# Attention's transfers pinned to program order and placed earlier, its memory branch a step later, token tiles in two stages

## The chip, the core and the metric

One core of a Trainium2 chip runs one program. The metric is device time in microseconds (us) of one execution, from launch to the end; lower is better. TensorE (PE) does matmuls, VectorE (DVE), ScalarE (ACT) and GpSimd (POOL) do the elementwise work, and SyncE (SP) issues almost every DMA transfer. Each engine works through its own queue in order.

## The reference, cut to what matters

```
q, k, v: [4, 8, 576, 64];  M_prev: [4, 8, 64, 64];  z_prev: [4, 8, 64]
scores = q k^T / 8, causal;  a = softmax(scores);  local = a v
phi(x) = where(x > 0, x, exp(x) - 1) + 1
mem_out = (phi(q) M_prev) / (phi(q) . z_prev + 1e-6)
x = g * mem_out + (1 - g) * local        # g = sigmoid(beta), per head
x = reshape(x) to [2304, 512]
x = relu(x w_in)^2 w_out                 # 512 -> 2048 -> 512
out = mixture of 8 experts over x        # each token to one expert, capacity 288
```

w_in and w_out arrive as 64-bit floats and are turned into 32-bit ones on the chip.

## The kernel before

Attention works on pairs of heads: 4 batches of 4 pairs, numbered n = 0 to 15. `step(n)`, for n = -2 to 16, has ten places u = 0 to 9 and carries several pairs at once: `trans` transposes the probabilities of pair n (at each u), `score` makes those of pair n + 1 (at u = 1, 3, 5, 7, 8), `prep_q` and `prep_k` split q and k of pair n + 2 into a high and a low part (u = 4 and 8), `prep_v` does so for v of pair n (u = 2), `prep_m` transposes phi(q) of pair n (u = 1 and 3), and `read` makes the attention output (the pair's first columns at u = 4 and 8, the rest at u = 0 and 1 of the next step, after which it is stored to `x_d` in DRAM). `PLAN` lists these places. `phi(n)` is the memory branch: two ACT instructions write `e`, one DVE instruction `qp`, POOL multiplies by `zb` (z_prev on all partitions), DVE reduces that to `nr`, POOL scales `qp`. The tiles `e`, `qp`, `zb`, k and v have one buffer each, q has two.

Between these pieces `fill` puts matmuls of the first pass over the feed-forward layer (`Ffn.first`), from step 4 on: `FILLS` and `BEFORE` say how many at each place, 60 in a whole step. That pass goes by 8 tiles of 288 tokens. `tokens(i)` loads tile i from `x_d` in four chunks of 128 features (`xf`, two buffers), POOL adds the two halves of each, ACT and DVE split it into `xs` (one buffer), and `xs` is stored to `xs_d` for the later passes. Then 72 matmuls make the hidden layer of 6 chunks (`hidden`), and 72 more the output in 4 pieces d (`output`), each of which ACT copies to `yo` (two buffers) and SP stores to `yp_d`. Tile i can begin when its batch has been stored (`ended` sets `have`): tiles 0 and 1 from step 4 on, 2 and 3 from step 8, 4 and 5 from step 12, 6 and 7 at the end. `CONVERT` puts two conversions of a weight chunk (`fetch`, then `narrow` and `split`) into each of steps 0 to 5.

PE follows the program's order. The order on the other engines, and on SP's queue, is set by a scheduler that walks the program with a model of the times and issues what is ready, earlier traced work first. `keep_in_program_order` ties one instruction behind the one traced before it on its engine. Before the change it is used for the weight fetches of the first pass and for the first ACT instruction of their conversion, and for nothing else: all other transfers go where the scheduler puts them. So `phi(n + 2)`, traced at u = 1 of step n, cannot write `qp` before `prep_m` of pair n + 1 has been through PE, a step later.

Of the kernel before, what the change touches and what calls it, by code (L numbers as in the profile page):

```python
# [7 lines left out]
F32 = mybir.dt.float32  # L8
# [20 lines left out]

def narrow(nc, f, tmp, raw):  # L30
# [5 lines left out]
    a = nc.scalar.activation(tmp.bitcast(F32), high.bitcast(F32), AF.Copy, scale=2.0 ** -112)  # L36
# [3 lines left out]
    return a  # L40
# [9 lines left out]
def attention(tc, ident, q, k, v, M_prev, z_prev, beta, x_d, fill, ended):  # L50
# [5 lines left out]
    with ExitStack() as ctx:  # L56
# [13 lines left out]
        def load(n, names="qkv"):  # L70
            b, hp = divmod(n, HP)
            for nm, src in (("q", q), ("k", k), ("v", v)):
# [4 lines left out]
                for j in range(2):  # L77
                    nc.sync.dma_start(dst[:, 0:4, j, :],
                                      src[b, 2 * hp + j, 0:512, :].rearrange("(t p) d -> p t d", p=128))
                for to, r in ends:  # L80
                    nc.sync.dma_start(to[r:r + 64, 4], src[b, 2 * hp:2 * hp + 2, 512:576, :].rearrange("h p d -> p h d"))
# [3 lines left out]
        nc.sync.dma_start(g, beta[None, :].to_broadcast([128, H]))  # L85
# [26 lines left out]
        MB, zb = {}, {}  # L112

        def load_norm(b):
            zb[b] = one.tile([128, DM], F32, name="zb")
            nc.sync.dma_start(zb[b], z_prev[b].rearrange("h d -> (h d)")[None, :].to_broadcast([128, DM]))

        def load_memory(n):
            b, hp = divmod(n, HP)
            raw = two.tile([128, 2, 64], F32, name="mraw")  # L120
            for j in range(2):
                nc.sync.dma_start(raw[64 * j:64 * j + 64], M_prev[b, 2 * hp:2 * hp + 2].rearrange("h d e -> d h e"))
            m = MB[n] = two.tile([128, 2, 128], F32R, name="mb")
            split(nc, m[:, :, 0:64], m[:, :, 64:128], raw)
# [41 lines left out]
        def phi(n):  # L166
            b, hp = divmod(n, HP)
            if hp == 0:
                load_norm(b)
# [8 lines left out]
                                    zb[b][:, None, 128 * hp:128 * hp + 128].to_broadcast([128, 5, 128]), op=OP.mult)  # L178
# [119 lines left out]
        def read(n, c, j):  # L298
# [18 lines left out]
            if c == 1 and j == 1:  # L317
                xo = XO.pop(n)
                for s in range(2):
                    nc.sync.dma_start(x_d[s, 128 * hp:128 * hp + 128, b * S:b * S + S].rearrange("(j d) t -> d j t", j=2),  # L320
                                      xo[64 * s:64 * s + 64])

        def step(n):
# [3 lines left out]
            for u in range(10):  # L327
                if has[1]:
                    trans(n, u)
# [4 lines left out]
                for what in PLAN[u]:  # L334
# [960 lines left out]
```

## Time and profile before

| | us |
|---|---|
| median of 3 runs | 1049.72 (1047.99 to 1050.88) |
| profiled execution, its own time | 1049.03 |
| span from first to last instruction in it | 1047.3 |
| attention's steps alone, until the first pass's matmuls join | about 0 to 120 |
| attention's steps with the first pass beside them | about 120 to 369 |
| rest of the first pass | about 369 to 424 |
| later passes, then the mixture of experts | 424 to the end |

The span is what the views below divide. What is outside it (1.7 us) is launch and end.

### The profile page before, as it was taken

The page shows a single profiled execution, that of the slowest core. Times are in us where ns is not written, and L with a number is a line of the kernel's source. Part 1 is how long each engine was busy: PE and PEld are TensorE (multiplying, and loading weights), DVE is VectorE, ACT ScalarE, POOL GpSimd, SP SyncE. Part 2 cuts the span into 40 slices and gives each one's busy share as a digit, 9 for nine tenths or more (in the row PEclk, how much of TensorE's full clock was granted, in tenths as well). Part 3 has the DMA queues.
Part 4 walks back from the last instruction along what each step waited for, and adds up shares of the span by engine and source line. Part 5 has one row for each costly group of instructions (what it writes and reads, how often), then busy time and mean ns, then how long its engine had stood idle before and what let it go on. Part 6 is the DMA issues. An engine that isn't in the chain of part 4 may idle for free.

```text
span 1047.3 us, 19732 instructions
## 1 busy us (share of the span) xinstructions
PE 959.4 (92%) x7017; PEld 879.1 (84%) x7017; DVE 655.2 (63%) x1925; ACT 552.6 (53%) x1370; POOL 540.3 (52%) x535
## 2 busy tenths in 40 slices
PE   5777879999999988999999999999598999999996
PEld 3666668988889987999999999877498888989996
DVE  6889888888888737256427943335775567674110
ACT  6778878888888735444322343431252453344531
POOL 4666776766666525344312121211394865687841
PEclk9778889999999999999999999999698999999999
DMA  6345736374526277769583332101542444437400
GB/s 154 106 123 142 192 89 179 75 196 100 172 67 175 56 233 227 220 223 315 185 293 122 117 125 83 68 12 41 193 162 79 152 184 151 156 130 258 147 28 27
DMA packets 150724, 150.75 MB, mean 144 GB/s; under 512 B 71641, under 2 KB 122841, under 8 KB 150497
## 3 DMA queue, kind: packets, MB, share of 16 engines
q1 hardware_dynamic: 147552, 140.05, 43.6%
q0 software_dynamic: 3072, 9.44, 2.9%
q8 instruction: 55, 0.90, 0.4%
q14 instruction: 45, 0.36, 0.1%
HBM read 111.69 MB, written 37.77 MB: 143 GB/s over the span
## 4 chain that ended last, share of the span: by engine, by line
PE 61%; DVE 12%; issue 7%; DMA 6%; ACT 6%; POOL 5%; SPq 1%; POOLq 0%; DVEq 0%; ACTq 0%
PE ph L1066 12%; PE ph L45 6%; PE ph L46 6%; PE ph L47 6%; PE py L45 4%; PE py L46 4%; PE py L47 4%; PE ps L312 3%; POOL wsp L1050 3%; PE ps L217 3%; PE ps L271 2%; PE rs L843 2%; DMA raw<-in_moe_w_out_dram 1%; DMA raw<-in_moe_w_in_dram 1%; ACT P L240 1%
## 5 line engine op out<-in xcount | busy, mean ns | idle before, releaser
L489 POOL TENSOR_TENSOR gf<-r 128x384 f32<-128x384 f32 (+1 forms) x108 | 87.4, 810 | 206.9 <-ACT r L487 198.1
L1050 POOL TENSOR_TENSOR wsp<-wraw,wsp 128x1024 fp32r<-128x1024 f32 x64 | 150.9, 2393 | 42.8 <-ACT wsp L1048 31.6
L26 DVE TENSOR_TENSOR gs<-gf,gs 128x384 fp32r<-128x384 f32 (+1 forms) x108 | 65.6, 607 | 91.4 <-ACT gs L25 90.9
L1066 PE MATMUL ph<-xs,wsp 128*128 128x288 f32 x768 | 120.0, 306 | 0.0
L1066 PE MATMUL ph<-hs,wsp 128*128 128x288 f32 x768 | 117.5, 307 | 0.0
L246 POOL TENSOR_SCALAR P<-P,R,og 128x128 f32<-128x128 f32 (+2 forms) x144 | 99.5, 707 | 24.6 <-DVE R L244 17.7
L1066 PEld LDWEIGHTS ph<-xs,wsp 128*128 128x128 f32 x768 | 106.6, 192 | 3.6 <-issue 2.8
L1066 PEld LDWEIGHTS ph<-hs,wsp 128*128 128x128 f32 x768 | 107.2, 194 | 0.9 <-DVE hs L1090 0.4
L1048 ACT ACTIVATE wsp<-wraw 128x1024 fp32r<-128x1024 f32 x64 | 64.0, 1051 | 48.6 <-DMA wraw<-in_moe_w_dram 29.1
L487 ACT ACTIVATE r<-ph 128x384 f32<-128x384 f32 (+1 forms) x108 | 48.6, 450 | 77.6 <-PE ph L47 76.5
L240 ACT ACTIVATE P<-P,R 128x128 f32<-128x128 f32 (+2 forms) x144 | 83.4, 580 | 8.4 <-DVE R L228 6.9
L25 ACT ACTIVATE gs<-gf 128x384 fp32r<-128x384 f32 (+1 forms) x108 | 52.5, 486 | 58.0 <-POOL gf L489 49.6
L45 PE MATMUL ph<-xt,win 128*128 128x384 f32 x240 | 81.3, 339 | 0.0
L46 PE MATMUL ph<-xt,win 128*128 128x384 f32 x240 | 80.8, 337 | 0.0
L47 PE MATMUL ph<-xt,win 128*128 128x384 f32 x240 | 80.7, 336 | 0.0
L45 PE MATMUL ph<-xs,win 128*128 128x288 f32 x192 | 64.3, 335 | 10.6 <-ACT r L487 7.6
L271 PE MATMUL ps<-ident,P 128*128 128x128 f32 x320 | 62.3, 302 | 8.6 <-DVE R L228 3.3
L46 PE MATMUL py<-gs,wout 128*128 128x384 f32 x192 | 64.7, 338 | 0.3 <-DVE gs L26 0.3
L47 PE MATMUL py<-gs,wout 128*128 128x384 f32 x192 | 63.9, 336 | 0.0
L26 DVE TENSOR_TENSOR ptb<-ps,ptb 128x384 fp32r<-128x384 f32 (+3 forms) x128 | 59.1, 464 | 7.4 <-ACT ptb L25 5.8
L45 PE MATMUL py<-gs,wout 128*128 128x384 f32 x192 | 63.4, 338 | 0.0
L228 DVE CUSTOM_DVE_ANT_0 P<-ps,maskw 128x128 f32<-128x128 f32 (+3 forms) x128 | 58.5, 483 | 6.2 <-PE ps L217 3.2
(259 smaller groups left out, 2596.4 us busy)
## 6 DMA issues: line engine op xcount, KB each, us to landing
wraw<-in_moe_w_dram SPq DMA_DIRECT2D x32, 1024.0 KB, 5.5
xt<-xs_d SPq DMA_DIRECT2D x12, 1536.0 KB, 7.2
x_d<-xo SPq DMA_DIRECT2D x32, 288.0 KB, 3.8
xf<-x_d SPq DMA_DIRECT2D x32, 288.0 KB, 3.8
xs_d<-xs SPq DMA_DIRECT2D x8, 1152.0 KB, 6.6
raw<-in_moe_w_in_dram SPq DMA_DIRECT2D x16, 512.0 KB, 5.4
raw<-in_moe_w_out_dram SPq DMA_DIRECT2D x16, 512.0 KB, 5.5
yp<-yo SPq DMA_DIRECT2D x32, 144.0 KB, 3.9
```

Of the source, the lines that this page charges most:

```text
L26: (eng or nc.vector).tensor_tensor(lo, src, hi.bitcast(F32), op=OP.subtract)
L45: nc.tensor.matmul(out, lhi, rhi, start=start, stop=False)
L46: nc.tensor.matmul(out, lhi, rlo, start=False, stop=False)
L47: nc.tensor.matmul(out, llo, rhi, start=False, stop=stop)
L228: nc.vector.tensor_tensor_reduce(out=pw, in0=ps[:, 0:W[u]], in1=maskw[:, 512 - 128 * t:640], op0=OP.add, op1=OP.min, scale=-0.125, scalar= ...
L240: nc.scalar.activation(pw, pw, AF.Exp, bias=R[:, 0, u:u + 1], scale=-1.0, accum_out=R[:, 1, u:u + 1])
L246: nc.gpsimd.tensor_scalar(PP[n][w], PP[n][w], R[:, 2, w:w + 1], og9[:, hp, w:w + 1], op0=OP.mult, op1=OP.mult)
L271: nc.tensor.transpose(tr[:, 128 * i:128 * i + 128], P[:, 128 * i:128 * i + 128], ident)
L489: nc.gpsimd.tensor_tensor(gf, r, r, op=OP.mult)
L1048: nc.scalar.activation(w[:, 0, hs], raw[:, hs], AF.Copy)
L1050: eng.tensor_tensor(w[:, 1, hs], raw[:, hs], w[:, 0, hs].bitcast(F32), op=OP.subtract)
L1066: nc.tensor.matmul(out, l[a], r[b], start=i + p == 0, stop=i == n - 1 and p == 2)
```

## The change

1. **Transfers pinned.** A helper `transfer` issues a DMA and ties it behind the SP instruction traced before it. It is used for the loads of q, k, v, beta, z_prev and M_prev, the store to `x_d`, and, as long as attention runs, for the loads of `xf` and the stores of `xs_d` and `yp_d`.
2. **Places.** The loads stood after the step; now q of pair n + 3 stands at u = 5, k at u = 6, v of pair n + 1 at u = 7, M_prev and z_prev of pair n + 1 at u = 0. The load of M_prev is apart from its split (`prep_memory`, u = 4).
3. **Memory branch.** `phi(n + 1)` stands at u = 4 where `phi(n + 2)` stood at u = 1.
4. **z_prev by pairs.** A tile of 128 columns per pair (16 loads) in place of one of 512 per batch (4 loads).
5. **Token tiles in two stages.** Stage 0 loads and adds chunks 0 and 1; stage 1 splits them, then loads, adds and splits chunks 2 and 3. For the next tile stage 0 stands after the fourth hidden chunk and stage 1 at the start of the output; where the batch is not stored by then, they stand at output pieces 2 and 3. Tile 0 does one, 4 calls of waiting, the other, 4 more. Before, the whole stood at output piece 2, tile 0's at the start with 8 calls of waiting. The store to `xs_d` moves behind the second hidden chunk.
6. **Conversions.** The first ACT instruction is no longer tied, it writes a buffer of its own (`rc`) instead of `r`, which the hidden layer uses too, and the first fetch stands in step -1.

```diff
+def transfer(tc, out, src, pinned=True):
+    a = tc.nc.sync.dma_start(out, src)
+    if pinned:
+        tc.keep_in_program_order(a)
...
-        MB, zb = {}, {}
-
-        def load_norm(b):
-            zb[b] = one.tile([128, DM], F32, name="zb")
-            nc.sync.dma_start(zb[b], z_prev[b].rearrange("h d -> (h d)")[None, :].to_broadcast([128, DM]))
+        MB, MR, zb = {}, {}, {}
+
+        def load_norm(n):
+            b, hp = divmod(n, HP)
+            zb[n] = one.tile([128, 128], F32, name="zb")
+            transfer(tc, zb[n], z_prev[b, 2 * hp:2 * hp + 2].rearrange("h d -> (h d)")[None, :].to_broadcast([128, 128]))
         def load_memory(n):
             b, hp = divmod(n, HP)
-            raw = two.tile([128, 2, 64], F32, name="mraw")
+            raw = MR[n] = two.tile([128, 2, 64], F32, name="mraw")
             for j in range(2):
-                nc.sync.dma_start(raw[64 * j:64 * j + 64], M_prev[b, 2 * hp:2 * hp + 2].rearrange("h d e -> d h e"))
+                transfer(tc, raw[64 * j:64 * j + 64], M_prev[b, 2 * hp:2 * hp + 2].rearrange("h d e -> d h e"))
+
+        def prep_memory(n):
             m = MB[n] = two.tile([128, 2, 128], F32R, name="mb")
-            split(nc, m[:, :, 0:64], m[:, :, 64:128], raw)
+            split(nc, m[:, :, 0:64], m[:, :, 64:128], MR.pop(n))
...
@@ step(n)
+                if u == 0 and has[2]:
+                    load_memory(n + 1)
+                if u == 0 and has[2]:
+                    load_norm(n + 1)
+                if u == 5 and n + 3 < np_:
+                    load(n + 3, "q")
+                if u == 6 and n + 3 < np_:
+                    load(n + 3, "k")
+                if u == 7 and has[2]:
+                    load(n + 1, "v")
...
-                    if what == "p" and has[3]:
-                        phi(n + 2)
+                    if what == "p" and has[2]:
+                        phi(n + 1)
                     if what == "q" and has[2]:
-                        load_memory(n + 1)
+                        prep_memory(n + 1)
...
-            if n + 3 < np_:
-                load(n + 3, "qk")
-            if 0 <= n + 1 < np_:
-                load(n + 1, "v")
...
-CONVERT = {0: (10, 0), 1: (10, 0), 2: (10, 0), 3: (10, 0), 4: (10, 0), 5: (4, 10)}
+CONVERT = {-1: (10,), 0: (10, 0), 1: (10, 0), 2: (10, 0), 3: (10, 0), 4: (10, 0), 5: (4, 10)}
-PLAN = (("b0",), ("b1", "m0", "p"), ("v",), ("m1",), ("q", "k0", "a0"), (), (), (), ("k1", "a1"), ())
+PLAN = (("b0",), ("b1", "m0"), ("v",), ("m1",), ("p", "q", "k0", "a0"), (), (), (), ("k1", "a1"), ())
...
@@ weights(...)
-        t_ = (psum or self.two).tile([128, DM], I32, name="pr" if psum and psum is self.p2x else "r")
+        if first:
+            t_ = self.start.tile([128, DM], I32, name="rc")
+        else:
+            t_ = (psum or self.two).tile([128, DM], I32, name="pr" if psum and psum is self.p2x else "r")
...
@@ tokens(i)
-        xs = self.start.tile([128, 2, KD, TB], F32R, name="xs")
-        for kk in range(KD):
-            xf = self.start.tile([128, 2, TB], F32, name=f"xf{kk % 2}")
-            nc.sync.dma_start(xf, self.x_d[:, 128 * kk:128 * kk + 128, TB * i:TB * i + TB].rearrange("s p t -> p s t"))
-            nc.gpsimd.tensor_tensor(xf[:, 0], xf[:, 0], xf[:, 1], op=OP.add)
-            split(nc, xs[:, 0, kk], xs[:, 1, kk], xf[:, 0])
-        nc.sync.dma_start(self.xs_d[:, :, :, TB * i:TB * i + TB], xs.bitcast(F32))
-        return xs
+        def load(ks):
+            for kk in ks:
+                xf[kk] = self.start.tile([128, 2, TB], F32, name=f"xf{kk % 2}")
+                transfer(self.tc, xf[kk], self.x_d[:, 128 * kk:128 * kk + 128, TB * i:TB * i + TB].rearrange("s p t -> p s t"),
+                         self.yout is None)
+                nc.gpsimd.tensor_tensor(xf[kk][:, 0], xf[kk][:, 0], xf[kk][:, 1], op=OP.add)
+        def parts(ks):
+            for kk in ks:
+                split(nc, xs[:, 0, kk], xs[:, 1, kk], xf[kk][:, 0])
+        xf = {}
+        load((0, 1))
+        yield
+        xs = self.xs[i] = self.start.tile([128, 2, KD, TB], F32R, name="xs")
+        parts((0, 1))
+        load((2, 3))
+        parts((2, 3))
+        yield
@@ first(gpool)
-        nc, xs, cs = self.nc, {}, PASSES[0]
+        nc, cs, at, way = self.nc, PASSES[0], [0] * (NB_T + 1), {}
+        def ahead(i, stage):
+            if i < NB_T and self.have > i and at[i] == stage:
+                way.setdefault(i, self.tokens(i))
+                next(way[i])
+                at[i] += 1
         for i in range(NB_T):
             while self.have <= i:
                 yield 0
-            if i not in xs:
-                xs[i] = self.tokens(i)
-                for _ in range(LAG):
+            while at[i] < 2:
+                ahead(i, at[i])
+                for _ in range(LAG // 2):
                     yield 0
-            G = {}
+            xs, G = self.xs[i], {}
             for c in cs:
-                G[c] = yield from self.hidden(xs[i], c, gpool)
+                G[c] = yield from self.hidden(xs, c, gpool)
+                if c == cs[1]:
+                    transfer(self.tc, self.xs_d[:, :, :, TB * i:TB * i + TB], xs.bitcast(F32), self.yout is None)
+                if c == cs[3]:
+                    ahead(i + 1, 0)
             for ds in ((0, 1), (2,), (3,)):
-                if ds[0] and i + 1 < NB_T and i + 1 not in xs and self.have > i + 1:
-                    xs[i + 1] = self.tokens(i + 1)
+                ahead(i + 1, 0 if ds[0] == 2 and not at[i + 1] else 1)
...
@@ apart(...)
-        raws = []
+        raws = [f.fetch(c, part, pool, f"raw{n}") for n, (part, c) in enumerate(todo[:1])]
+        yield
```

## Rows read from the trace of the kernel before

**Rows 1.** Page: span, then busy us, share and instructions of each engine.

```profile
span 1047.3 us, 19732 instructions
PE 959.4 (92%) x7017; PEld 879.1 (84%) x7017; DVE 655.2 (63%) x1925; ACT 552.6 (53%) x1370; POOL 540.3 (52%) x535
```

**Rows 2.** Windows: length, busy (instructions) PE, PEld, DVE, ACT, POOL; granted clock; DMA.

```profile
26.90:112.60 85.70, 67.64 (x399) 54.44 (x398) 78.66 (x226) 70.13 (x203) 58.02 (x66) 0.81 0.47 125
112.60:146.60 34.00, 22.64 (x144) 18.88 (x143) 28.32 (x74) 23.72 (x69) 29.27 (x33) 0.82 0.68 179
146.60:318.90 172.30, 168.90 (x1274) 151.98 (x1273) 143.65 (x431) 146.24 (x446) 110.44 (x141) 1.00 0.48 126
...
369.00:425.00 56.00, 47.85 (x334) 45.83 (x333) 30.26 (x47) 25.46 (x60) 25.36 (x28) 0.97 0.75 237
```

**Rows 3.** Timeline of PE (start, us): prep_q's transposes at u = 4, five of sixteen.

```profile
112.58 0.60 PE L131 MATMUL ps<-ident,nq 128*128 128x128 f32 x4
146.59 1.05 PE L131 MATMUL ps<-ident,nq 128*128 128x128 f32 x4
...
233.68 0.60 PE L131 MATMUL ps<-ident,nq 128*128 128x128 f32 x4
254.17 0.60 PE L131 MATMUL ps<-ident,nq 128*128 128x128 f32 x4
...
318.85 0.60 PE L131 MATMUL ps<-ident,nq 128*128 128x128 f32 x4
```

**Rows 4.** Waits of ACT, 10 to 360 us: total, times, longest.

```profile
ACT e L172 <- DVE nr L180: 13.6, 10, 2.6
```

**Rows 5.** Timeline of ACT, step 5 (in brackets: idle before, releaser).

```profile
142.44 0.74 ACT L172 ACTIVATE e<-nq 128x640 f32<-128x640 f32 x1 [2.24 <-DVE nr L180]
...
143.84 0.65 ACT L36 ACTIVATE r<-raw 128x512 f32<-128x512 f32 x1
144.51 0.41 ACT L487 ACTIVATE r<-ph 128x288 f32<-128x288 f32 x1
```

**Rows 6.** Timeline of PE in steps 4 and 5: hidden-layer matmuls that waited.

```profile
124.55 0.40 PE L46 MATMUL ph<-xs,win 128*128 128x288 f32 x1 [0.72 <-DVE xs L26]
...
144.98 0.61 PE L45 MATMUL ph<-xs,win 128*128 128x288 f32 x1 [6.65 <-ACT r L487]
```

**Rows 7.** Timeline of PE, steps 8 to 10: places u = 6, 7, 3 and 4.

```profile
237.93 0.60 PE L271 MATMUL ps<-ident,P 128*128 128x128 f32 x4
239.57 0.60 PE L271 MATMUL ps<-ident,P 128*128 128x128 f32 x4
...
250.09 0.38 PE L271 MATMUL ps<-ident,P 128*128 128x128 f32 x2
...
254.96 0.36 PE L304 MATMUL ps<-qpt,mb 128*128 128x256 f32 x1
```

**Rows 8.** Timeline of SP, first token chunks and the end of attention.

```profile
56.58 0.59 SPq L473 DMA_DIRECT2D xf<-x_d  x1
...
367.21 0.55 SPq L476 DMA_DIRECT2D xs_d<-xs  x1
...
369.58 1.26 SPq L539 DMA_DIRECT2D xt<-xs_d  x1
```

**Rows 9.** Page, DMA issues: count, KB, median us from issue to landing.

```profile
xf<-x_d SPq DMA_DIRECT2D x32, 288.0 KB, 3.8
...
nv<-in_v_dram SPq DMA_DIRECT2D x32, 128.0 KB, 3.3
```

**Rows 10.** Instructions on tile xf: min/median/max ns.

```profile
L474 POOL TENSOR_TENSOR xf<-xf x32: 795/807/1395, 59.9 to 421.9; 128x288 f32<-128x288 f32 x32
```

**Rows 11.** Timeline of ACT after attention: output copies that waited for a store.

```profile
374.16 0.41 ACT L526 ACTIVATE yo<-ph 128x288 f32<-128x288 f32 x1 [4.41 <-DMA yp<-yo]
...
383.09 0.41 ACT L526 ACTIVATE yo<-ph 128x288 f32<-128x288 f32 x1 [2.58 <-DMA yp<-yo]
```

**Rows 12.** Waits in SP's queue, whole span: total, times, longest.

```profile
SPq L122 <- DVE mb L26: 40.1, 6, 9.4
```

More of the change, by code (lines that the diff above doesn't have):

```diff
@@ L27, in split @@
     return a.ins
+def transfer(tc, out, src, pinned=True):
+    a = tc.nc.sync.dma_start(out, src)
+    if pinned:
+        tc.keep_in_program_order(a)
 def narrow(nc, f, tmp, raw):
     low, high = raw[..., 0], raw[..., 1]
[L36 removed]
+    nc.scalar.activation(tmp.bitcast(F32), high.bitcast(F32), AF.Copy, scale=2.0 ** -112)
     nc.vector.tensor_scalar(f, tmp, 3, None, op0=OP.logical_shift_left)
@@ L77, in load @@
                 for j in range(2):
-                    nc.sync.dma_start(dst[:, 0:4, j, :],
-                                      src[b, 2 * hp + j, 0:512, :].rearrange("(t p) d -> p t d", p=128))
+                    transfer(tc, dst[:, 0:4, j, :], src[b, 2 * hp + j, 0:512, :].rearrange("(t p) d -> p t d", p=128))
                 for to, r in ends:
-                    nc.sync.dma_start(to[r:r + 64, 4], src[b, 2 * hp:2 * hp + 2, 512:576, :].rearrange("h p d -> p h d"))
+                    transfer(tc, to[r:r + 64, 4], src[b, 2 * hp:2 * hp + 2, 512:576, :].rearrange("h p d -> p h d"))
         load(0, "qk")
         g = one.tile([128, H], F32, name="g")
-        nc.sync.dma_start(g, beta[None, :].to_broadcast([128, H]))
+        transfer(tc, g, beta[None, :].to_broadcast([128, H]))
         maskw = one.tile([128, 640], F32, name="maskw")
@@ L177, in phi @@
             nc.gpsimd.tensor_tensor(e.rearrange("p (t c) -> p t c", t=5), qp.rearrange("p t j d -> p t (j d)"),
-                                    zb[b][:, None, 128 * hp:128 * hp + 128].to_broadcast([128, 5, 128]), op=OP.mult)
+                                    zb[n][:, None, :].to_broadcast([128, 5, 128]), op=OP.mult)
             nr = two.tile([128, 5, 2], F32, name="nr")
@@ L319, in read @@
                 for s in range(2):
-                    nc.sync.dma_start(x_d[s, 128 * hp:128 * hp + 128, b * S:b * S + S].rearrange("(j d) t -> d j t", j=2),
-                                      xo[64 * s:64 * s + 64])
+                    transfer(tc, x_d[s, 128 * hp:128 * hp + 128, b * S:b * S + S].rearrange("(j d) t -> d j t", j=2),
+                             xo[64 * s:64 * s + 64])
         def step(n):
@@ L414, in __init__ @@
         nc.vector.tensor_tensor(self.two8, ident[0:16, 0:8], ident[0:16, 8:16], op=OP.add)
-        self.win, self.wout, self.Y, self.have = {}, {}, {}, 0
+        self.win, self.wout, self.Y, self.xs, self.have = {}, {}, {}, {}, 0
     def fetch(self, c, part, pool, name="raw"):
@@ L438, in weights @@
         raw = self.fetch(c, part, pool) if raw is None else raw
-        t_ = (psum or self.two).tile([128, DM], I32, name="pr" if psum and psum is self.p2x else "r")
+        if first:
+            t_ = self.start.tile([128, DM], I32, name="rc")
+        else:
+            t_ = (psum or self.two).tile([128, DM], I32, name="pr" if psum and psum is self.p2x else "r")
         held = part and c >= PASSES[-1][0]
         f_ = (self.two if first else self.keep if held else pool).tile([128, DM], I32, name="gf")
-        a = narrow(nc, f_, t_, raw.rearrange("p (n t) -> p n t", t=2))
-        if first:
-            self.tc.keep_in_program_order(a)
+        narrow(nc, f_, t_, raw.rearrange("p (n t) -> p n t", t=2))
         split(nc, dst[:, 0], dst[:, 1], f_.bitcast(F32), eng)
@@ L526, in first @@
                             nc.scalar.activation(yo, py[d], AF.Copy)
-                            nc.sync.dma_start(self.yp_d[0][i][128 * d:128 * d + 128], yo)
+                            transfer(self.tc, self.yp_d[0][i][128 * d:128 * d + 128], yo, self.yout is None)
     def later(self, gpool, beside, turn):
```

3 lines of the change are left out of this document (removed).

## The prediction

> **What bounds the kernel now.** The page comes first. PE is busy for 92% of the span and every other engine for less than two thirds [rows 1], but that is a mean over stages with different limits, and this change touches only the part before 425 us. So the windows are read next, cut where the stages change [rows 2].
>
> Until 112.6 us attention runs alone. DVE is busy for 78.7 of 85.7 us (92%), PE's clock is at 0.81 and PE is no limit. From 146.6 to 318.9 us PE is busy for 168.9 of 172.3 us at full clock. Between them lie 34 us in which no engine is full: POOL 29.3, DVE 28.3, PE 22.6. After attention, from 369 to 425 us, PE lacks 56.0 - 47.9 = 8.1 us and nothing else is near full; the DMA engines carry 237 GB/s.
>
> A step's length is read from PE's timeline, at the transposes of q, which come once in each step [rows 3]. From 233.68 to 254.17 a step takes 20.49 us, the shortest full one. From 146.59 to 318.85 eight take 172.26 us, 21.5 each. So 172.26 - 8 x 20.49 = 8.3 us in this stage are above the shortest step. The one step from 112.58 to 146.59 takes 34.0 us, 13.5 above it. These 13.5, 8.3 and 8.1 us, and what DVE leaves idle before 112 us (85.7 - 78.7 = 7.0), are all that the change could win.
>
> Who holds these steps up is read from ACT's waits. The first instruction of the memory branch waits for the last reader of tile `e`: ten times, 13.6 us in all [rows 4]. The timeline shows one case whole [rows 5]: at 142.44 ACT has stood for 2.24 us behind this wait, while the relu of a finished hidden chunk was queued behind it; the relu starts at 144.51, and PE, which wants its bank back, has waited 6.65 us [rows 6]. The branch was put there by the scheduler, since it was traced a step early.
>
> **The change part by part.** The sum is made against the profiled execution, 1049.0 us (span 1047.3 and 1.7 around it), 0.7 under the median of 1049.7; the forecast adds the 0.7 again.
>
> *Memory branch at u = 4 for the next pair.* It has the same instructions, and they run about where they ran, since `qp` has one buffer and was free only after u = 3. What goes is ACT's wait: `e` has been free for most of a step when the branch comes. Of the 13.6 us, 2.24 lie in step 5, and give PE back up to about 4 of its 6.65 us (the relu also stood behind L172, L173 and a conversion, 142.44 to 144.51). Before 112 us DVE is the limit and I take 1 us. In the PE-bound stage I take half of the 8.3 us: 4. Bounds: nothing if other work fills ACT at once, the whole 8.3 if the waits were all of it. What is late next is `qp`, needed at u = 1 of the next step, about seven places on.
>
> *Transfers pinned and earlier.* In the middle stage no transfer is waited for by PE, so this wins nothing there. It costs nothing while each transfer has slack. v of pair n + 1 is issued from u = 7 (239.57) and read at u = 4 of the next step (254.96 for the same pair of places): 15.4 us [rows 7]. Four issues of 0.6, as one of rows 8, take 2.4, landing 3.3 [rows 9], and the two splits 2.5 (an estimate: ACT as L172, 0.74 for 640 columns [rows 5]; POOL 0.81 x 640 / 288 by rows 10). That leaves 7.2 us. q and k have more. At the very start v of pair 0 now queues behind q and k of pair 2, which wait for the first memory branch; I take 1 us lost, between 0 and 3.
>
> *z_prev by pairs.* Twelve more transfers, each a quarter of the size. Twelve issues of 0.6 are 7 us on SP, spread over twelve steps of over 20 us: 0 us as long as SP has 0.6 us to spare in a step, 7 us if it never has, and I take 0, since v's slack alone is ten times that.
>
> *Token tiles.* Chunks 0 to 2 of tile 0 were fetched while attention ran alone, the first at 56.58 [rows 8], and PE waited only 0.72 us for the last one [rows 6]. Now tile 0 starts in step 4. The three splits leave the DVE-bound stage (each between the 0.41 of an ACT copy of this shape [rows 5] and POOL's 0.81 [rows 10], so 1.2 to 2.4 us; I take 1.5 won), but stage 1 gets its chunks late. From its place to a split chunk it takes 1 us until the yo store and the issue are through, 3.8 to land [rows 9], 0.81 on POOL [rows 10], 1 for the splits, and 1 to 1.5 us in each queue of three: 10 to 11 us. In step 4 the first hidden matmuls follow three places later, so PE waits about 5 us, in a step whose other engines have work to catch up with. I charge 3 us of it, between 0 and 6. Tile 2, whose batch is stored late, does stages 0 and 1 at pieces 2 and 3. From u = 3 (250.09) plus 1.5 us of matmuls to u = 6 of the same step (237.93 + 20.49 = 258.42) there are 6.8 us [rows 7]: a wait of 2 to 4 us; I charge 2.5. Tiles 1 and 3 to 7 have the whole output before them and win nothing, since PE does not wait for them now.
>
> *The step of 34 us.* It wins 4 by the branch and loses 3 by tile 0. It also wins by the `rc` buffer, which frees the relu's buffers from the conversions, but POOL takes two more adds, 29.3 + 1.6 = 30.9 us of work, so at most 3 us are there in all. Net 1 us won, between 3 won and 6 lost.
>
> *After attention.* ACT stood twice for a store to free `yo`, 4.41 and 2.58 us [rows 11], PE with it. The queue shows why: the last loads of tile 5, the store of the whole `xs` tile and the prefetch `xt` were issued between and ahead of those stores [rows 8]. Now tile 5 is loaded a place earlier and its `xs_d` store comes after its second hidden chunk, while `xt` and the next weights stay. I take half of the 7.0 us: 3.5, between 0 and 7.
>
> The sum: before 112 us 1 + 1.5 - 1 = 1.5; step 4 to 5 1.0; middle 4 - 2.5 = 1.5; after attention 3.5. That is 7.5 us won, less 1 us for a new order on DVE, ACT and POOL that nothing of before can tell: 6.5. 1049.7 - 6.5 = 1043.2, rounded to 1043. From 425 us on nothing is touched.
>
> **The rivals.** *Nothing to be seen.* PE does its 168.9 of 172.3 us whoever waits beside it, DVE its 78.7, and only the half after attention comes, 3.5 us, less the 2.5 us of tile 2: 1048 to 1050. For it: PE shows hardly any idle time in the middle. Against it: the eight steps of equal work are 1.0 us longer on the mean than the shortest of them.
>
> *Slower by late token tiles.* The one mechanism: stage 1's second pair of chunks is fetched only when it is needed. It decides once the chain of 10 us is longer than the gap to its matmul, 6.8 us at tile 2, and the waits of tiles 0 and 2 are not absorbed: 6 + 4 us, and up to 3 more where PE's clock falls after such a wait, as it has in the 34 us step (mean 0.82 [rows 2]): 10 to 13 us, less 4 to 5 won elsewhere: 1054 to 1058. For it: 0.72 us was left at tile 0 with three chunks prepared.
>
> *Slower by the queue.* With one order for all transfers, one that is not ready holds all behind it. The longest wait in SP's queue is 9.4 us, the six of its kind 6.7 on average [rows 12]; 9.4 is 2.2 more than v's slack of 7.2. Six steps with it lose 13 us, less 6.5 won: about 1056, and 1063 without the gains. Against it: the new places come after what they wait for. The Trainium skill (DMA: Bandwidth & Descriptors, in the section Anatomy of one DMA) states the rule behind this: a wait on a semaphore happens on the sequencer that issues, before dispatch, not in the DMA engines. By that rule every pinned transfer inherits the waits of those ahead of it, and the time would be this rival's; the trace agrees as far as its 9.4 us go.
>
> **How the numbers follow.** What a measurement of this kernel can tell from no change is 0.3%, 3.1 us. The forecast has 0.50, with 1035 to 1046 as its own range; nothing to be seen 0.23; late tiles 0.17; the queue 0.10. The range leaves out the far ends: half of the lowest case would need all bounds at once. From 1034 (the gains of all parts at about two thirds of their bounds) to 1056 (the middle of the slow cases). Faster 0.50, same 0.23, slower 0.27.
>
> **What would show it.** Right: no wait of L172 for L180 on ACT; the step of 34 us at 31 to 35; the steps after it at 21.0 to 21.4; the waits of `yo` for stores at half. Wrong: hidden-layer matmuls of tile 0 or 2 that wait for `xs` by over 5 us; vt or `zb` waiting for their loads; steps before 112 us longer than 21.4 us, which would be the unknown order.

## The result and the profile after

| | us |
|---|---|
| kernel after, median of 4 runs | 1059.36 (1058.83 to 1061.81) |
| kernel before beside it, median of 4 runs | 1048.86 (1044.15 to 1050.88) |
| ratio | 1.0111, 95% interval 1.0073 to 1.0149 |
| profiled execution after: own time, span | 1058.83, 1057.1 |

The change makes the kernel slower by 10.5 us. The forecast was 1043, and the time lies above the range. Run again the ratio was 1.0118 (f1 below).

The page of the kernel after, span and PE (columns as in [rows 1]):

```profile
span 1057.1 us, 19744 instructions
PE 968.1 (92%) x7017; PEld 884.6 (84%) x7017; DVE 647.9 (61%) x1925; ACT 556.0 (53%) x1370; POOL 537.6 (51%) x535
```

PE does the same 7017 matmuls as in [rows 1] and is busy for 8.7 us longer, so some of them ran at a lower clock. Where time was lost PE's timeline shows, at the q transposes of steps 4, 5, 9, 10, 11 and 13 (those of [rows 3], and one more):

```profile
115.59 0.60 PE L139 MATMUL ps<-ident,nq 128*128 128x128 f32 x4
148.29 0.60 PE L139 MATMUL ps<-ident,nq 128*128 128x128 f32 x4
...
238.14 0.60 PE L139 MATMUL ps<-ident,nq 128*128 128x128 f32 x4
265.16 0.60 PE L139 MATMUL ps<-ident,nq 128*128 128x128 f32 x4
290.88 0.60 PE L139 MATMUL ps<-ident,nq 128*128 128x128 f32 x4
...
332.98 0.60 PE L139 MATMUL ps<-ident,nq 128*128 128x128 f32 x4
```

The last group stands 14.1 us later than in [rows 3]. The step from 4 to 5 takes 32.7 us instead of 34.0; but the step from 9 to 10, before the shortest of those from 5 on with 20.5, takes 27.0, and the next one 25.7. The windows of these stretches (columns as in [rows 2]):

```profile
30.86:115.60 84.74, 67.39 (x398) 53.73 (x398) 73.99 (x223) 68.80 (x197) 55.62 (x65) 0.84 0.48 115
115.60:148.30 32.70, 25.14 (x144) 20.74 (x143) 24.67 (x66) 23.00 (x67) 19.52 (x23) 0.79 0.55 141
148.30:174.50 26.20, 23.46 (x162) 20.36 (x161) 21.16 (x61) 21.19 (x62) 20.73 (x26) 0.93 0.61 169
174.50:238.10 63.60, 62.14 (x479) 56.33 (x477) 51.78 (x161) 53.53 (x162) 40.53 (x51) 1.00 0.48 119
238.10:265.20 27.10, 24.61 (x162) 21.33 (x161) 18.92 (x56) 19.82 (x60) 14.09 (x20) 0.87 0.55 147
265.20:290.90 25.70, 23.16 (x161) 20.37 (x160) 20.33 (x60) 19.43 (x59) 16.43 (x21) 0.93 0.43 110
```

In the two late steps PE has a lower clock (0.87 and 0.93 where [rows 2] had 1.00) and idle time as well. The stages before step 4 are as long as before from 30.9 us on; what they lost they lost earlier, in the step from -1 to 0, which ends at 30.9 instead of 26.9 us. That step takes 14.3 to 14.9 us in the runs below that have neither the memory branch a step later nor the untied conversions, and 16.2 to 18.9 in all that have either.

All runs can be put into one table. Its times are differences between q transposes (u = 4 of the steps named) in each kernel's profiled execution; the ratio is to the kernel before on the same chip, whose median was between 1046 and 1058 us by chip. e9 to e12, g1 and g2 had 1057 and 1058, where the expectations in us reckoned with about 1048, so results are held against them as ratios. These two chips lose the difference behind attention: from the last q transposes to the end of the span their profiles take 732 to 741 us, all others 724 to 729.

| run | ratio (95%) | step -1 to 4 | 4 to 6 | 6 to 9 | 9 to 11 | 11 to 13 |
|---|---|---|---|---|---|---|
| before | | 100.6 | 55.5 | 65.6 | 42.4 | 42.8 |
| after | 1.0111 (1.0073 to 1.0149) | 103.5 | 58.9 | 63.6 | 52.8 | 42.1 |
| f1 after again | 1.0118 (1.0089 to 1.0148) | 106.4 | 61.0 | 61.9 | 49.5 | 42.2 |
| e1 | 1.0125 (1.0074 to 1.0176) | 110.5 | 52.4 | 67.7 | 43.3 | 42.7 |
| e2 | 1.0090 (1.0059 to 1.0122) | 97.2 | 62.2 | 61.8 | 50.6 | 41.1 |
| e3 | 1.0150 (1.0101 to 1.0199) | 107.0 | 56.8 | 61.9 | 50.4 | 42.1 |
| e4 | 1.0053 (1.0027 to 1.0079) | 105.9 | 55.8 | 65.9 | 42.6 | 42.8 |
| e5 | 1.0060 (1.0030 to 1.0090) | 98.7 | 57.3 | 63.2 | 50.9 | 41.9 |
| e6 | 1.0058 (1.0033 to 1.0084) | 109.4 | 50.8 | 66.0 | 42.8 | 42.0 |
| e7 | 1.0049 (1.0025 to 1.0072) | 101.5 | 56.1 | 66.7 | 45.1 | 41.0 |
| e8 | 1.0065 (1.0038 to 1.0092) | 106.8 | 53.9 | 67.9 | 42.8 | 42.6 |
| e9 | 1.0003 (0.9976 to 1.0029) | 106.2 | 54.1 | 65.3 | 42.7 | 41.9 |
| e10 | 1.0117 (1.0079 to 1.0155) | 103.1 | 61.2 | 67.5 | 42.3 | 41.6 |
| e11 | 1.0008 (0.9987 to 1.0029) | 100.6 | 55.5 | 66.2 | 42.4 | 42.5 |
| e12 | 1.0096 (1.0059 to 1.0134) | 109.2 | 55.9 | 64.5 | 44.8 | 41.9 |
| f2 | 1.0066 (1.0043 to 1.0089) | 98.4 | 60.9 | 61.9 | 49.6 | 42.1 |
| f3 | 1.0112 (1.0092 to 1.0133) | 102.5 | 56.4 | 63.0 | 49.2 | 41.1 |
| f4 | 1.0083 (1.0066 to 1.0099) | 109.6 | 56.7 | 65.2 | 42.5 | 42.8 |
| g1 | 1.0048 (1.0014 to 1.0082) | 104.1 | 53.5 | 65.2 | 44.1 | 42.1 |
| g2 | 1.0020 (0.9987 to 1.0053) | 106.9 | 57.8 | 65.5 | 42.7 | 41.9 |

A column of single executions is to be read with care. The kernel after and f1 are one program, and differ by 2.9 us in the first column. The column 9 to 11, however, has two clear kinds of rows, and they go with one edit: the loads of the token tiles are tied in the seven runs with 49.2 us or more.

### The profile page after: what moved, and what is told of

It reads as the page before. It is cut to its first block, busy times and chain, and to the rows that moved or that the text cites. A ratio compares the mean times of both kernels' runs of the same rounds, so it can differ in the third digit from the quotient of the medians.

```text
span 1057.1 us, 19744 instructions
## 1 busy us (share of the span) xinstructions
PE 968.1 (92%) x7017; PEld 884.6 (84%) x7017; DVE 647.9 (61%) x1925; ACT 556.0 (53%) x1370; POOL 537.6 (51%) x535
## 4 chain that ended last, share of the span: by engine, by line
PE 61%; DVE 11%; DMA 8%; issue 7%; ACT 6%; POOL 5%; SPq 2%; POOLq 0%; ACTq 0%; DVEq 0%
PE ph L1101 12%; PE ph L51 7%; PE ph L52 6%; PE ph L53 6%; PE py L51 4%; PE py L52 4%; PE py L53 4%; POOL wsp L1085 3%; PE ps L223 3%; PE ps L318 2%; PE rs L878 2%; PE ps L277 2%; DMA xf<-x_d 2%; SPq L32 2%; DMA raw<-in_moe_w_out_dram 1%
## 5 line engine op out<-in xcount | busy, mean ns | idle before, releaser
L1085 POOL TENSOR_TENSOR wsp<-wraw,wsp 128x1024 fp32r<-128x1024 f32 x64 | 150.9, 2388 | 41.1 <-ACT wsp L1083 40.8
L26 DVE TENSOR_TENSOR gs<-gf,gs 128x384 fp32r<-128x384 f32 (+1 forms) x108 | 62.6, 580 | 91.1 <-ACT gs L25 90.5
L252 POOL TENSOR_SCALAR P<-P,R,og 128x128 f32<-128x128 f32 (+2 forms) x144 | 96.7, 684 | 24.4 <-DVE R L250 17.1
L1083 ACT ACTIVATE wsp<-wraw 128x1024 fp32r<-128x1024 f32 x64 | 64.0, 1051 | 50.2 <-DMA wraw<-in_moe_w_dram 32.5
L246 ACT ACTIVATE P<-P,R 128x128 f32<-128x128 f32 (+2 forms) x144 | 83.3, 580 | 10.5 <-DVE R L234 8.9
L26 DVE TENSOR_TENSOR ptb<-ps,ptb 128x256 fp32r<-128x256 f32 (+3 forms) x128 | 59.7, 467 | 12.0 <-ACT ptb L25 10.1
```

The costliest lines, as they stand in the source:

```text
L26: (eng or nc.vector).tensor_tensor(lo, src, hi.bitcast(F32), op=OP.subtract)
L246: nc.scalar.activation(pw, pw, AF.Exp, bias=R[:, 0, u:u + 1], scale=-1.0, accum_out=R[:, 1, u:u + 1])
L252: nc.gpsimd.tensor_scalar(PP[n][w], PP[n][w], R[:, 2, w:w + 1], og9[:, hp, w:w + 1], op0=OP.mult, op1=OP.mult)
L1083: nc.scalar.activation(w[:, 0, hs], raw[:, hs], AF.Copy)
L1085: eng.tensor_tensor(w[:, 1, hs], raw[:, hs], w[:, 0, hs].bitcast(F32), op=OP.subtract)
```

## The experiments

**The token tiles.** The first theory was the rival of the forecast: the two stages fetch the second pair of chunks too late.

e1, the kernel after with `tokens` and `first` as in the kernel before:

```diff
-        load((0, 1)); yield; parts((0, 1)); load((2, 3)); parts((2, 3)); yield
+        for kk in range(KD): (load, add, split)      # one piece, transfers untied
```

> The kernel after, with the token tiles loaded and prepared as before (one piece, its transfers not tied), all else as after. Late token chunks: steps 5 to 6, 9 to 10 and 10 to 11 go back from 26.2, 27.0 and 25.7 us to 21 to 22, and the time falls by 10 to 15 us, to 1045 to 1049. Rival, attention's tied transfers hold the steps up (head of the queue): those steps stay long, and the time stays at 1056 to 1060.

e2, the kernel before with the new `tokens` and `first`, their transfers pinned:

> The kernel before, with the token tiles of after alone (two stages, their transfers and the stores of the first pass tied). Late token chunks: the steps in which tiles 1, 2 and 3 are prepared grow by 4 to 6 us each, 1058 to 1064. Rival (the tied loads of attention): within 3 us of before.

e2 is slower by 0.9% and has the long steps 9 to 11; e1 has them short, and is no faster than the kernel after, so neither theory holds whole. (In its one profile the first column is the longest of all; that this is the reason is not shown.) So the tiles make the late steps long, but their undoing alone doesn't bring the time back.

What is late in them? SP's queue in the kernel after, around the loads of tile 2 (start and length of an issue):

```profile
227.15 0.97 SPq L32 DMA_DIRECT2D xf<-x_d  x2
...
234.58 1.25 SPq L32 DMA_DIRECT2D x_d<-xo  x2
237.46 0.34 SPq L32 DMA_DIRECT2D yp<-yo  x1
237.90 0.95 SPq L32 DMA_DIRECT2D xf<-x_d  x2
```

The same kernel's timelines of DVE (the last split of the first pair), ACT (the copy that the store `yp` waits for) and PE (the matmuls that want the second pair):

```profile
233.62 0.57 DVE L26 TENSOR_TENSOR xs<-xf,xs 128x288 fp32r<-128x288 f32 x1
...
237.03 0.41 ACT L561 ACTIVATE yo<-ph 128x288 f32<-128x288 f32 x1
...
243.98 0.40 PE L51 MATMUL ph<-xs,win 128*128 128x288 f32 x1 [0.77 <-ACT xs L25]
245.40 0.40 PE L52 MATMUL ph<-xs,win 128*128 128x288 f32 x1 [1.02 <-DVE xs L26]
...
246.63 0.61 PE L51 MATMUL ph<-xs,win 128*128 128x288 f32 x1 [0.70 <-ACT xs L25]
```

The buffers of the second pair were free at 234.19. Its issue came at 237.90, 3.7 us later, directly behind the store of `x_d`, which SP held until 234.58, and the store `yp`, whose `yo` was ready at 237.44. PE then waited three times, 0.77, 1.02 and 0.70 us. The last row shows the rest of the price: the same matmul takes 0.61 us instead of 0.40. The windows of this stretch (columns as in [rows 2]) have the granted clock at 1.00 and then at 0.51, so from about 246 to 253 us PE is at the lower of its two levels, 1.2 GHz in place of 2.4:

```profile
238.10:246.20 8.10, 6.04 (x43) 4.92 (x41) 7.65 (x19) 6.61 (x18) 5.84 (x9) 1.00 0.86 221
246.20:253.00 6.80, 6.37 (x24) 4.98 (x25) 3.00 (x8) 2.53 (x7) 1.32 (x2) 0.51 0.65 203
```

The fall goes with the tie. It comes at 239 to 251 us in all seven profiles with tied loads; in the other thirteen the clock never falls between 225 and 320 us.

e6, the kernel after with these transfers left to the scheduler, the two stages kept:

```diff
-    (xf loads, xs_d and yp stores)  transfer(..., self.yout is None)
+    (xf loads, xs_d and yp stores)  transfer(..., False)
```

> The kernel after, with its token tiles still in two stages, but their transfers (xf, xs_d, yp) left to the scheduler instead of kept in program order. Theory A, the two stages cost by themselves, because the second pair of chunks is fetched only after the first pair is split: the two steps from 238 to 291 us stay at 52 to 53 us together (43 in the kernel before) and the time at 1057 to 1061. Theory B, it is the pinned place of these transfers in SP's queue that delays them: the two steps come back to 43 to 45 us and the time to 1050 to 1053.

Measured 1051.38 us, ratio 1.0058. Theory B holds. SP's timeline and the windows of the two late steps of e6:

```profile
221.97 0.89 SPq L32 DMA_DIRECT2D xf<-x_d  x2
...
228.13 0.37 SPq L32 DMA_DIRECT2D xf<-x_d  x1
...
232.13 1.54 SPq L32 DMA_DIRECT2D xf<-x_d  x1
```

```profile
238.20:258.90 20.70, 20.70 (x161) 18.91 (x160) 16.88 (x54) 18.39 (x58) 13.78 (x20) 1.00 0.38 94
258.90:281.00 22.10, 21.37 (x161) 18.98 (x160) 19.21 (x58) 18.43 (x57) 14.91 (x19) 1.00 0.51 138
```

Against the q transposes of step 8 (214.8 us here, 217.29 in the kernel after) the four chunks are issued at 7.2, 7.2, 13.3 and 17.3 us, instead of 9.9, 9.9, 20.6 and 20.6. PE's 161 matmuls take 20.70 us at full clock, and 24.61 for 162 at 0.87: of the 6.4 us between the two steps 3.9 are slower matmuls and 2.5 PE's idle time (27.10 - 24.61, none in e6).

e11, the kernel before with the two stages alone, untied:

> The kernel before with the token tiles in two stages, but none of their transfers kept in program order (with them kept in order this was 1057.5 us). Theory A, the order of the queue and not the two stages made them slow: 1043 to 1048, with 42 to 44 us for the two late steps that took 50.6 there, and no hidden matmul waiting for xs by over 2 us in them. Theory B, the two stages by themselves cost: 1053 to 1058.

Ratio 1.0008: no loss, and the late steps at 42.4 us. Against e2 (1.0090) only the order of the queue differs.

e12 unties the loads alone, f3 the stores alone, both in the kernel after:

> The kernel after, where of the token tiles' transfers only the loads of the chunks (xf) are left to the scheduler; the stores xs_d and yp keep their program order. Theory A, it is the loads that have to stand behind the store of x_d and the next pair's transfers: 1050 to 1053, as with all three kinds untied (1051.4), and 43 us for the two late steps. Theory B, it is the pinned stores that hold everything: 1057 to 1060, and 52 us for those steps.

> The kernel after, where the stores xs_d and yp of the token tiles are left to the scheduler and the loads xf keep their program order. In the trace of after the second pair of chunks of tile 2 is issued right behind the store yp, which waits for its yo until 237.4 us, while its buffers were free some 4 us earlier. Theory A, that store is what holds the loads: the two late steps at 43 to 46 us and a ratio of 1.004 to 1.008. Theory B, the loads' own place is what counts, since x_d and q, k, v stand ahead of them too: the two late steps at 50 to 53 us and a ratio of 1.009 to 1.013.

SP's timeline, the two pairs of tile 2, first in e12, then in f3:

```profile
225.48 0.89 SPq L32 DMA_DIRECT2D xf<-x_d  x2
...
231.51 1.56 SPq L32 DMA_DIRECT2D xf<-x_d  x2
```

```profile
223.02 0.96 SPq L32 DMA_DIRECT2D xf<-x_d  x2
...
230.37 1.25 SPq L32 DMA_DIRECT2D x_d<-xo  x2
233.25 0.34 SPq L32 DMA_DIRECT2D yp<-yo  x1
233.70 0.95 SPq L32 DMA_DIRECT2D xf<-x_d  x2
```

From the q transposes of step 8 these are 7.2 and 13.2 us in e12 (218.3), 9.8 and 20.5 in f3 (213.2). It is the loads' own tie that makes them late, and the late steps go with it: 44.8 and 49.2 us. Which store holds them f3 doesn't tell: a tied load stands behind whatever was traced ahead of it, tied or not, so `x_d` and `yp` are still directly ahead of the second pair, as in the kernel after. In time, e12 was not measurably faster than the kernel after (1.0096, where Theory A expected what e6 has); its first column is long, and a single profile can't tell why. So the late steps are shown to come from the tie of the loads, and the 0.5 to 0.8% from the ties of all three kinds together (e6; e11 beside e2).

**The conversions.** e5, the kernel after with them as before; f2, only ACT's instruction tied again, with `rc` and the early fetch kept:

```diff
-        narrow(nc, f_, t_, raw.rearrange("p (n t) -> p n t", t=2))
+        a = narrow(nc, f_, t_, raw.rearrange("p (n t) -> p n t", t=2))
+        if first:
+            self.tc.keep_in_program_order(a)
```

> The kernel after, with the weight conversions of attention's time as they were before: no chunk fetched ahead in the step before pair 0, no own buffer rc, and the ACT instruction kept in program order. In the kernel after the step from the second to the third group of q transposes takes 18.8 us and in the kernel before 14.9; a conversion runs in it, at 16.8 to 22.3 us on ACT and DVE, that ran at 30 us before. Theory A, the early conversion is what lengthens it: this step comes back to about 15 us and the time to 1055 to 1056. Theory B, the pinned loads or the memory branch lengthen it: the step stays at 18 to 19 us and the time at 1058 to 1061.

> The kernel after, where ACT's first instruction of each weight conversion is kept in program order again; the buffer rc and the chunk fetched ahead stay. With all of the conversions' part undone the ratio fell from 1.011 to 1.006. Theory A, the conversions cost because they may run early, into the first steps: here 1.004 to 1.008. Theory B, the buffer or the early fetch costs, or that difference was the clock of those runs: 1.009 to 1.014.

f4, the kernel before with the tie removed and the first chunk fetched early:

> The kernel before with the conversions' part alone, as far as it fits: the first chunk fetched in the step before pair 0, and ACT's instruction not kept in program order; the buffer r stays shared. Theory A, early conversions cost by themselves: a ratio of 1.004 to 1.008, and the step that took 14.9 us at 16 to 19. Theory B, they cost only beside the pinned loads and the later branch: 0.998 to 1.003.

e5 1.0060, f2 1.0066 (1054.0 us beside 1060.2 for f1), f4 1.0083, just over its range: by the ratios Theory A in all three, and `rc` and the early fetch are not what costs the kernel after. But the place that e5's expectation named was wrong. The step from -1 to 0 doesn't come back to 15 us: it stays at 17.6 us in e5 and 18.5 in f2 (18.9 in f4). The step from 0 to 1 is 17.2 in e5, e9, f2, g1 and g2, all with the tie, and 18.3 to 21.7 in the seven runs of the changed kernel without it (20.4 in five of them, the kernel after and f1 among them; 26.6 in f4). Both steps together take 39.2 us in the kernel after and 38.9 in f1, 34.5 to 35.7 in those five with the tie, and 34.1 in the kernel before. DVE in that step, the kernel after:

```profile
30.99 0.79 DVE L44 TENSOR_SCALAR gf<-rc 128x512 int32<-128x512 int32 x1
...
32.06 0.88 DVE L45 SCALAR_TENSOR_TENSOR rc<-rc,gf 128x512 int32<-128x512 int32 x1
...
33.23 0.95 DVE L46 SCALAR_TENSOR_TENSOR gf<-raw,rc 128x512 int32<-128x512 int32 x1
34.10 0.54 DVE L26 TENSOR_TENSOR ptb<-ps,ptb 128x384 fp32r<-128x384 f32 x1
...
36.98 0.82 DVE L186 TENSOR_REDUCE nr<-e 128x10 f32<-128x640 f32 x1
```

PE and POOL in the same step:

```profile
34.79 0.88 PE L277 MATMUL ps<-ident,P 128*128 128x128 f32 x3 [1.05 <-DVE ptb L26]
...
33.61 1.97 POOL L183 TENSOR_TENSOR e<-qp,zb 128x640 f32<-128x640 f32 x1
```

and DVE in f2 (its lines are one further down):

```profile
30.07 0.82 DVE L187 TENSOR_REDUCE nr<-e 128x10 f32<-128x640 f32 x1
...
34.69 0.43 DVE L44 TENSOR_SCALAR gf<-rc 128x512 int32<-128x512 int32 x1
...
35.54 0.68 DVE L45 SCALAR_TENSOR_TENSOR rc<-rc,gf 128x512 int32<-128x512 int32 x1
...
37.09 0.89 DVE L46 SCALAR_TENSOR_TENSOR gf<-raw,rc 128x512 int32<-128x512 int32 x1
```

Untied, the conversion may run as soon as its weights have landed, and its 0.79 + 0.88 + 0.95 = 2.6 us of DVE stand ahead of `ptb`, for which PE waits 1.05 us, in the stage that DVE bounds. Tied, they come behind `nr`. `nr` itself is later in the kernel after for another reason: it needs POOL's product `e`, which ends at 35.58, after the conversion has left DVE (34.18). How the 3.2 us of this step add up is not shown beyond that; that the tie makes them is, by f2.

**Both undone.** e9 has e5's and e6's edits together; g2 has f2's and e6's, g1 f2's and e12's.

> The kernel after, with both edits undone that measured faster than it by themselves: the weight conversions as before (1053.2 us alone) and the token tiles' transfers left to the scheduler (1051.4 us alone). The two stages of the token tiles, the pinned transfers of attention, z_prev by pairs and the memory branch at u = 4 stay. Theory A, the two costs lie in different steps and add up: 1059.4 - 6.2 - 8.0 = 1045, which is 1 us under the kernel before or equal to it. Theory B, both only let the same stall move, which another part brings back: 1050 to 1053.

> The kernel after with two edits: ACT's first instruction of each conversion kept in program order, as in the kernel before, and the loads xf of the token tiles left to the scheduler; the stores yp and xs_d stay in program order. The first edit alone measured 1.0066. Theory A, the place of the loads is what costs: the late steps at 43 to 46 us and a ratio of 0.998 to 1.003. Theory B, the pinned stores cost as much elsewhere, in the steps of tile 0 or after attention: 1.004 to 1.008, and under 1.003 only in the run that unties them too.

> The same with the stores yp and xs_d left to the scheduler too. The buffer rc, the early fetch, z_prev by pairs, the branch at u = 4 and the pinned transfers of attention all stay. Both theories: 0.997 to 1.003; over 1.004 would mean that rc or the early fetch costs as well, since with the whole of the conversions' part undone it was 1.0003.

e9 1.0003, g2 1.0020, g1 1.0048. Taken as ratios, 1.0111 less 0.0051 (e5) less 0.0053 (e6) is 1.0007: the two costs add up. They are the whole loss of the kernel after, within the interval of e9 (0.9976 to 1.0029). Whether the pinned stores cost anything beside the loads is not settled: the intervals of g1 and g2 overlap, and g1, with the loads alone untied, is not measurably under f2 (1.0066) either. No version measured faster than the kernel before.

**The memory branch, the pins and z_prev.** e4, e8 and e7 are the kernel before with one edit each:

```diff
-                    if what == "p" and has[3]:
-                        phi(n + 2)
+                    if what == "p" and has[2]:
+                        phi(n + 1)          # e4: "p" moved to u = 4 in PLAN; e8: left at u = 1
```

> The kernel before, with the memory branch of the next pair at u = 4 and nothing else. If ACT's wait behind it was what lengthened the step of 34 us and the PE-bound steps, 1041 to 1046; if PE and DVE limit these stages whoever waits, or the order changes, 1048 to 1051.

> The kernel before, with the memory branch traced for the next pair instead of the one after it, as the change does, but left at u = 1 instead of u = 4. The same edit at u = 4 measured 1052.9 us, 5 above the kernel before; its four unfilled steps took 105.9 us from the second group of q transposes on, before 100.6. Theory A, it is the place that costs, where the branch's DVE and ACT work stands ahead of the second half of a step's softmax: here 1046 to 1049, with about 101 us for those steps. Theory B, tracing it a step later costs by itself, because the scheduler no longer fills idle places with it: 1051 to 1054, with 104 to 107 us.

> The kernel before, with the transfers of attention (q, k, v, M_prev, beta, x_d) kept in program order at their new, earlier places, and nothing else of the change; z_prev stays one transfer for a batch, untied, and the memory branch and the token tiles stay as they were. Theory A, the prediction's: each transfer has slack, so the order costs nothing: 1046 to 1050. Theory B, one order for all transfers holds back those behind a late one: 1052 to 1057, with the step from the second to the third group of q transposes at 18 us or more instead of 14.9.

Ratios 1.0053, 1.0065 and 1.0049. The branch costs 0.5 to 0.7% alone, at either place, more than both values that e4's expectation allowed: that it stands at u = 4 is not the reason, that it is traced a step later is. The pins alone cost 0.5%, the time of Theory B, but the step it named takes 14.3 us, and no other single step shows the cost.

e3 is the kernel after with z_prev of pair 0 loaded ahead of q and k of pair 1. In the kernel after POOL had waited for it:

```profile
15.41 1.53 POOL L183 TENSOR_TENSOR e<-qp,zb 128x640 f32<-128x640 f32 x1 [10.69 <-DMA zb<-in_z_prev_dram]
```

> The kernel after, with z_prev of pair 0 loaded ahead of q and k of pair 1. Late z_prev at the start: POOL's wait of 10.7 us for it goes to about 5, the transposes of q in step 0 come at 27 to 28 us in place of 30.9, and the time falls by 3 to 4 us, to 1055 to 1056. Rival (the early conversion of a weight chunk lengthens that step): 1058 to 1060.

1.0150: POOL's wait is gone (the same product starts at 9.64 us), but the q transposes of step 0 come at 31.2 us, not at 27 to 28, while those of step -1 now come at 13.4 instead of 12.1. The time is no lower. This theory fell.

e10 is e9 with the branch back at u = 1 for the pair after next and `zb` untied:

> The kernel of the run before this one with the memory branch back at u = 1 for the pair after next, too (z_prev by pairs stays, untied, since it has one buffer). The branch alone, put into the kernel before, cost 5 to 7 us. Theory A, it costs that in every context: 4 to 6 us under the run before this one, 1039 to 1042. Theory B, its cost was an order of the scheduler in the kernel before alone: within 2 us of the run before this one.

1.0117 against 1.0003 on the same chip, the opposite of Theory A: beside pinned transfers the old branch costs 1.1%. (The untied `zb` with its one buffer came with it and is not told apart.)

f1, the kernel after once more:

> The kernel after once more, unchanged, on the same chip as the three kernels of this call. Both theories: 1.008 to 1.014 of the kernel before, with 50 to 53 us for the two late steps (from the q transposes of the ninth step to those of the eleventh).

1.0118, and 49.5 us from 9 to 11, just short of the 50 to 53 expected.

## Why the prediction was wrong

**Where the sum failed.** Its parts can be held against the profiled executions of the kernel after and f1, by the q transposes. Before step 4 it had 1.5 us won; 3.0 and 5.9 were lost. From 4 to 5 it had 1.0 won; 1.3 and 1.5 were. From 5 to 13 it had 1.5 won; 12.4 and 9.8 were lost. Behind that it had 3.5 won, after attention; 4.3 and 0.4 were. Three steps of the prediction failed. The 9 us that the memory branch should win did not come (e4). The chain of the token tiles has 1 us "until the yo store and the issue are through"; at tile 2 that was 3.7 us, and the tied transfers of these tiles cost 0.5 to 0.8% (e6; e2 beside e11). The "new order on DVE, ACT and POOL", put at 1 us, cost 5 to 6 us by the untied conversions alone (f2, e5).

**Memory branch at u = 4** (4 + 4 + 1 us won): nothing of it shows. In e4 the steps from 6 to 13 take 151.2 us, before 150.7. The 8.3 us by which these steps are longer than the shortest one were not ACT's wait, and taking half of them for it had no row behind it. In the 34 us step the branch did what was forecast and more: in e4 it takes 26.1 us. But the next one takes 29.7, before 21.5, so the two together are no shorter (55.8, before 55.5). Beside the pinned transfers the branch, with the untied `zb`, makes 1.1% (e9 against e10), but that only makes up for them. Nor did the wait go, which the forecast made the first sign:

```profile
ACT e L178 <- DVE nr L186: 8.2, 8, 1.6
```

It was 13.6 us, ten times [rows 4].

**Token tiles** (1.5 won, 3 and 2.5 lost): the waits themselves were sized about right. In the kernel after PE waits 2.5 us for tile 2, as charged, and 3.6 for tile 0, where 3 were charged:

```profile
125.73 0.40 PE L51 MATMUL ph<-xs,win 128*128 128x288 f32 x1 [2.26 <-ACT xs L25]
...
127.44 0.61 PE L52 MATMUL ph<-xs,win 128*128 128x288 f32 x1 [1.31 <-DVE xs L26]
```

The sign of being wrong that was named here, a wait of over 5 us, did not come. What failed was the first term of the chain, 1 us until the store `yo` and the issue are through: from free buffers on it was 3.7 us at tile 2. What the term left out was the clock, 3.9 us of slower matmuls behind the 2.5 us wait (the rival had it, with up to 3), and tile 3. The prediction has tiles 1 and 3 to 7 without a loss; the step from 10 to 11, where tile 3 is prepared, takes 25.7 us in the kernel after and 23.5 in f1, before 21.9. The two late steps lost 7 to 10 us, of which 2 to 4 come back in the steps ahead of them (6 to 9: 61.8 to 63.6 us with tied loads, 64.5 to 67.9 without). What is left is of the size of the 0.5% that e6 gains. For tile 3 it was POOL that stood behind the chunks; the timelines of POOL, DVE and PE in the kernel after:

```profile
278.25 0.82 POOL L489 TENSOR_TENSOR xf<-xf 128x288 f32<-128x288 f32 x1 [2.58 <-DMA xf<-x_d]
280.19 0.79 POOL L489 TENSOR_TENSOR xf<-xf 128x288 f32<-128x288 f32 x1 [1.11 <-DMA xf<-x_d]
281.07 0.24 POOL L249 TENSOR_SCALAR R<-R 128x5 f32<-128x5 f32 x1
...
281.34 0.19 DVE L250 RECIPROCAL R<-R 128x5 f32<-128x5 f32 x1 [1.88 <-POOL R L249]
281.80 0.42 DVE L26 TENSOR_TENSOR ptb<-ps,ptb 128x256 fp32r<-128x256 f32 x1
...
282.27 0.55 PE L223 MATMUL ps<-kt,qt 64*128 64x128 f32 x5 [1.37 <-DVE ptb L26]
```

POOL's small instruction on `R` queued behind two adds whose data had not landed (2.58 and 1.11 us). DVE stood for 1.88 us for `R`, with `ptb` in its queue behind it, and PE for 1.37 us for `ptb` (0.71 in f1). The forecast compared tile 2's chain with its gap, and left out the adds' place in POOL's queue.

**The rivals.** Late token tiles (0.17) came nearest the time, 1054 to 1058. Its mechanism is half of the truth: the second pair is late, but not because it is fetched only when needed, for e11 fetches it so and loses nothing. It is the tie, the mechanism of the third rival (0.10), which named v of the next pair. By the rule that the third rival cited from the Trainium skill (DMA: Bandwidth & Descriptors, in the section Anatomy of one DMA), a wait is served on the issuing sequencer; the trace agrees, with 3.7 us between free buffers and the issue of `xf`.

**Conversions**: here the prediction failed without a sum. It counted only the freed `r`, and left what the new order on DVE, ACT and POOL may do at 1 us. The untied instruction is part of the change, is free to run early, and lies in the stage whose bound, DVE, the first paragraph had named. It costs 5 to 6 us (f2 beside f1, e5), and with the early fetch 8.7 in the kernel before (f4: 0.83% of 1046).

**Transfers pinned** (0, and 1 lost at the start) and **z_prev by pairs** (0): with the two costs above taken out, what stays of the change (pins, pairs, branch, two stages) measures as nothing, 1.0003. Alone the pins cost 0.5% and the branch 0.5 to 0.7%, which the prediction's method, slack by slack, could not see. One sign of being wrong that it named came: `zb` is waited for by 10.69 us at the start, before by 5.02. But e3 took that wait away, and the time stayed. The parts do not add: e2, e4, e7 and f4 sum to 2.75%, the whole change is 1.1%.

**The step of 34 us**: 32.7 and 32.5 us, within the 31 to 35, but by luck: the branch alone makes it 26.1 (e4, 4 us won in the sum) and the pinned tiles alone 39.6 (e2, 3 us lost). And the stall went into the next step, 26.2 and 28.5 us where 21.0 to 21.4 was expected: 4 to 6 takes 58.9 and 61.0 us, before 55.5.

**After attention** (3.5 won): one store is waited for by `yo`, where [rows 11] had two of 4.41 and 2.58 us:

```profile
397.48 0.41 ACT L561 ACTIVATE yo<-ph 128x288 f32<-128x288 f32 x1 [2.90 <-DMA yp<-yo]
```

That is the half of the wait that was forecast. From the last q transposes to the end of the span the kernel after takes 724.1 us, before 728.4, but f1 728.0: a gain of that size is not shown.

**Still open.** Why the branch and the pins cost 0.5% each alone and nothing together; why e1 and e12, with short late steps, are no faster than the kernel after; whether `x_d` or `yp` holds the tied loads; what makes up the rest of the conversions' 5 to 6 us beside the step from 0 to 1.

## What to carry to other kernels

When a load is tied to program order, look at every store ahead of it: it inherits the wait for their data, and a transfer that the scheduler used to bring forward loses that lead, here 3 us for the first pair and 3 to 7 for the second. When a tie is removed, ask what becomes ready first and which engine it will occupy: background work that may run early can land in the stage that can least bear it, as it did here. Test such a bundle part by part and also in pairs, since here four parts alone summed to two and a half times the whole.

## What the runs showed of the hardware

One program can run at different granted clocks in the same stretch. The kernel after and f1 are one program; the step from 2 to 3 in the one and in the other:

```profile
74.60:95.20 20.60, 16.89 (x102) 13.54 (x101) 18.08 (x57) 17.41 (x52) 12.88 (x16) 0.83 0.53 128
```

```profile
72.30:97.80 25.50, 20.21 (x101) 16.25 (x100) 18.40 (x57) 19.17 (x57) 17.09 (x19) 0.72 0.52 126
```

The matmuls are the same (102 and 101 records), DVE has 18.1 and 18.4 us to do, and the step takes 20.6 us at a clock of 0.83 and 25.5 at 0.72. PE's busy time makes 3.3 of these 4.9 us; the rest is idle time, and whether the clock or a wait came first is not shown. So in the steps before the first pass joins a difference of 5 us between two profiles is no evidence; that is why the causes above rest on ratios of several runs and on signatures that all profiles with an edit share.

A short wait cost about as much through the clock as by itself, or more. In the step from 9 to 10 PE had run at full clock from step 6 on; then 2.5 us of idle time went with 3.9 us of slower matmuls in the kernel after, and 2.7 with 2.5 in f1 (23.27 us of PE against e6's 20.74 in this step).
